# First-layer scores in the spare PSUM bank of the second layer's running state

## The chip, the cores and the metric

The kernel runs on one core of one Trainium2 chip. The metric is the time of one execution on the device in microseconds. Five engines matter. TensorE appears twice in the profile: PE is the streaming of a matmul and PEld the loading of its weights, which may overlap the matmul before it. DVE is VectorE, ACT is ScalarE, POOL is GpSimd, and SP issues the transfers. Products are written to PSUM, and here only ACT and DVE read them from there.

## The reference, cut to what matters

Four layers follow one another on 2048 tokens of width 576: attention A, experts B, A again, B again, with the same weights both times.

```
x = x + A(layernorm(x));  x = x + B(layernorm(x))      # "layer 0" of the kernel
x = x + A(layernorm(x));  x = x + B(layernorm(x))      # "layer 1" of the kernel

A:  q, k, v = x @ wqkv, 32 heads of 18;  pq, pk = phi(q), phi(k)
    kv = sum over tokens of pk (x) v;  z = sum over tokens of pk      # the running state
    o = (pq @ kv) / (pq . z);  return o @ wo
B:  q1, q2 = halves of x @ w_q (32 heads);  s1, s2 = q1 @ k1, q2 @ k2   # 8 scores each
    expert = (argmax s1, argmax s2), one of 64;  act = gelu(x . u[expert])
    return sum over heads of act * v[expert]
```

A is linear attention: its state `kv` needs keys and values of all tokens before the first output. The experts' scores are linear in x, so the kernel folds `w_q` with the keys once and gets the scores of a token by one product with a 576 x 512 matrix.

## The kernel before, in words

The tokens are cut into 16 tiles of 128. Every product of the big matrices is done in three parts, high x high, high x low and low x high, so an input is first transposed on TensorE and then split: ACT copies the high part out of PSUM (`thi`, L110), DVE subtracts it from the original for the low part (`tlo`, L111). The last letter of a name tells whose input it is: `thib`/`tlob` for the experts, `thif`/`tlof` for the next attention, `thio`/`tloo` for the attention's output.

For each token tile the pieces of a layer are small Python generators, and the order in which they run is written out by hand, first as a text that `play` reads, then for tiles 5 to 12 as a loop over `step2`, then as a text again. `in_order` makes this the order of each of PE, ACT, DVE and POOL. In the middle of the program the second half of layer 0 and the first half of layer 1 are interleaved. One `step2(s)` does on PE, in this order:

- `ppk`, `ppv` (L220): keys and values of layer 1, tile s-3
- `ptb` (L205): transposes of the experts' input of tile s and of the chosen experts' weights `cg` of tile s-1
- `ptf` (L205): transposes of layer 1's input of tile s-2
- `kva` (L291): 20 small products that add tile s-3 to layer 1's running state
- `pto` (L205): transposes of the attention's output of tile s+1
- `pps` (L444): the scores of tile s, 14 products of 512 columns, of which 5 have `thib` and `shi`, 4 `thib` and `slo`, and the last 5 `tlob` and `shi`
- `po` (L528): the experts' output of tile s-1
- `ppo` (L414): the attention's output product of tile s+1

`exp_scores` (L437 to L450) holds the scores: it takes a PSUM tile, runs the 14 products into its first 512 columns, and ACT copies these to `s` in SBUF (L449).

All PSUM tiles come from one pool of four slots. A slot is 1024 floats per partition, that is two banks of 512. The tile framework gives a new tile a slot that is free in its own order, and makes the new tile's first product wait until all readers of the slot's last tile have finished. `kva[1]`, the running state of layer 1, is allocated by `front_state(1, 0)` and kept until `state_mask(1)` has read it; its products touch columns 0 to 323, so the second bank of its slot is never written. While it lives three slots rotate among the other tiles. In `step2` eight tiles pass through three slots, so each takes the slot of the tile three before it: `pps` that of `ptb`, `po` that of `ptf`, `ppo` that of `pto`, and the next `ppk` that of `pps`.

Of the kernel before, what the change touches and what calls it, by code (L numbers as in the profile page):

```python
# [39 lines left out]
def blocks(rem):  # L40

    rows, at = [], 0
    for b in range(NB):
        rows.append((at, b - (b > rem)))
        at += 64 if b == rem else P
    return rows


def passes(rem):
    rest = [b for b in range(NB) if b != rem]  # L50
    return ([("hi", b, "hi") for b in range(NB)] + [("hi", b, "lo") for b in rest]
            + [("lo", b, "hi") for b in range(NB)])
# [6 lines left out]
def network(ctx, tc, x_in, wqkv, wo, wq_t, k_t, u_t, v2, c_mask, c_mask4, c_ident, c_code, c_code1, c_scale, c_shift, out):  # L59
# [7 lines left out]
    def psum(name):  # L67
        return ps.tile([P, 1024], F32, tag="ps", name=name)
# [165 lines left out]
    kva = {}  # L234
# [202 lines left out]
    def exp_scores(l, t):  # L437
        n = f"{l}_{t}"

        hl = tt.pop(("b", l, t))  # L440
        p = psum("pps" + n)
        todo = passes(REM)
        for i, (a, b, w) in enumerate(todo):
            nc.tensor.matmul(p[:, :512], hl[a == "lo"][:, b, :], shi[:, b] if w == "hi" else slo[:, blocks(REM)[b][1]],  # L444
                             start=(i == 0), stop=(i == len(todo) - 1))
        s = wk.tile([P, D], F32, tag="s", name="s" + n)
        nc.gpsimd.memset(s[:, :NE], 0.0)
        yield
        nc.scalar.activation(s[:, NE:], p[:, :512], AF.Copy)  # L449
        tt["s", l, t] = s  # L450
# [220 lines left out]
    wl, mk, zs, M = wo_load, state_mask, state_sum, state_fold  # L671
    ld, num, oT, O = back_load, back_scale, back_oT, back_out
    S, sel, gel, po = exp_scores, exp_select, exp_gelu, exp_out
    L = NT - 1

# [187 lines left out]
```

## Time and profile before

| | us |
|---|---|
| median of 3 runs (lowest to highest) | 747.09 (745.76 to 747.62) |
| profiled execution | 748.71 |
| its span, first to last instruction | 746.9 |
| PE busy / PEld busy in the span | 726.5 / 675.2 |
| DVE / ACT / POOL busy | 458.9 / 289.7 / 200.4 |
| granted TensorE clock, mean | 0.995 of full speed |

Layer 1's state is alive from about 298 us (first `kva` product of layer 1) to 533 us. The loop over `step2` takes from 309 to 451 us; one step is 17.7 us. In a row of a view `kva<-ek,v` is the tile written and the tiles read, `x5` the number of instructions put together, and the bracket at the end the time for which the engine stood idle before it and what ended that. Matmul ends are modelled from sizes, so starts are more exact than ends. The profile leaves out layer and tile numbers: `pps` is the scores of any tile.

### The profile page before, as it was taken

How to read it: one execution, taken by the hardware profiler on the slowest of the kernel's cores; microseconds unless marked ns; L12 is line 12 of the kernel's file. 1: busy time of each engine (PE TensorE's matmuls, PEld its weight loads, DVE VectorE, ACT ScalarE, POOL GpSimd, SP SyncE). 2: the span in 40 equal slices, each digit the busy share in tenths (PEclk: the TensorE clock that was granted, in tenths of full speed). 3: DMA queues.
4: the chain of work that ended last, by engine and by line, in shares of the span. 5: the costliest groups of instructions: out<-in, count | busy, mean ns of one | idle time of the engine just before them, and what ended most of it. 6: DMA issues, size and time to landing. Idle time of an engine off the chain costs nothing.

```text
span 746.9 us, 14647 instructions
## 1 busy us (share of the span) xinstructions
PE 726.5 (97%) x5672; PEld 675.2 (90%) x5672; DVE 458.9 (61%) x1006; ACT 289.7 (39%) x588; POOL 200.4 (27%) x541
## 2 busy tenths in 40 slices
PE   7999999999999999999999999999999999999995
PEld 4999999999998889999999999999899999999884
DVE  3732332324236887666666666563366899999986
ACT  4523232332324544444444444452233333444343
POOL 2110001000003543333333333130033334533431
PEclk9999999999999999999999999999999999999998
DMA  9727546641121321222333212222634323121101
GB/s 256 251 81 247 197 159 216 232 130 50 49 64 32 111 99 68 99 86 83 89 104 105 87 68 84 84 72 68 176 87 119 104 83 116 32 88 41 48 33 65
DMA packets 52470, 79.64 MB, mean 107 GB/s; under 512 B 5616, under 2 KB 22512, under 8 KB 52400
## 3 DMA queue, kind: packets, MB, share of 16 engines
q1 hardware_dynamic: 52400, 78.70, 33.1%
q8 instruction: 45, 0.74, 0.4%
q14 instruction: 25, 0.20, 0.1%
HBM read 55.12 MB, written 23.56 MB: 105 GB/s over the span
## 4 chain that ended last, share of the span: by engine, by line
PE 82%; DVE 10%; ACT 3%; issue 2%; POOL 1%; DMA 1%; SPq 0%; DVEq 0%; POOLq 0%; ACTq 0%
PE ppk L220 15%; PE ppv L220 15%; PE ppq L220 13%; PE ppo L414 13%; PE pps L444 12%; PE kva L291 3%; PE fold_ps L560 2%; PE ptb L205 2%; PE ptf L205 2%; PE pto L205 2%; PE po L528 2%; DMA wst<-in_wqkv 1%; PE m L345 1%; DVE o L392 1%; DVE tlob L111 1%
## 5 line engine op out<-in xcount | busy, mean ns | idle before, releaser
L227 DVE TENSOR_SCALAR ek<-ek 128x576 f32<-128x576 f32 x32 | 15.1, 472 | 82.5 <-ACT ek L226 82.5
L220 PE MATMUL ppk<-whi,thif 128*128 128x252 f32 x320 | 50.3, 302 | 2.4 <-ACT thif L110 2.3
L220 PEld LDWEIGHTS ppk<-whi,thif 128*128 128x128 f32 x320 | 44.6, 191 | 6.8 <-ACT thif L110 3.4
L414 PE MATMUL ppo<-ohi,thio 126*128 126x252 f32 (+1 forms) x320 | 50.2, 299 | 0.1
L171 POOL TENSOR_SCALAR rsf<-mvf 128x1 f32<-128x1 f32 x16 | 3.1, 192 | 171.2 <-DVE mvf L169 171.0
L220 PE MATMUL ppk<-whi,tlof 128*128 128x252 f32 x320 | 48.2, 295 | 0.3 <-DVE tlof L111 0.3
L227 DVE TENSOR_SCALAR eq<-eq 128x576 f32<-128x576 f32 x32 | 15.6, 488 | 52.5 <-ACT eq L226 52.5
L220 PE MATMUL ppv<-whi,thif 128*128 128x252 f32 x320 | 47.4, 294 | 0.1
L220 PE MATMUL ppv<-whi,tlof 128*128 128x252 f32 x320 | 46.9, 293 | 0.0
L195 ACT ACTIVATE yb<-x,rsb 128x640 f32<-128x640 f32 x32 | 29.5, 923 | 44.3 <-POOL rsb L188 44.2
L444 PE MATMUL pps<-shi,thib 128*128 128x512 f32 x160 | 43.9, 404 | 2.0 <-ACT thib L110 2.0
L414 PEld LDWEIGHTS ppo<-ohi,thio 126*128 126x128 f32 (+1 forms) x320 | 44.8, 189 | 1.1 <-DVE eq L228 0.3
L220 PEld LDWEIGHTS ppk<-whi,tlof 128*128 128x128 f32 x320 | 44.9, 190 | 0.5 <-DVE tlof L111 0.5
L220 PEld LDWEIGHTS ppv<-whi,thif 128*128 128x128 f32 x320 | 43.9, 188 | 0.4 <-ACT thif L110 0.3
L220 PEld LDWEIGHTS ppv<-whi,tlof 128*128 128x128 f32 x320 | 43.9, 188 | 0.0
L181 ACT ACTIVATE junk<-x,mb 128x576 bf16<-128x576 f32 x32 | 24.7, 771 | 49.5 <-POOL mb L180 46.1
L444 PE MATMUL pps<-shi,tlob 128*128 128x512 f32 x160 | 42.7, 397 | 0.0
L449 ACT ACTIVATE s<-pps 128x512 f32<-128x512 f32 x32 | 19.1, 596 | 54.9 <-PE pps L444 54.9
L251 ACT ACTIVATE v<-ppv 128x252 f32<-128x252 f32 x64 | 20.9, 379 | 50.0 <-PE ppv L220 50.0
L220 PE MATMUL ppq<-whi 128*128 128x252 f32 (+1 forms) x260 | 39.6, 299 | 0.6 <-DVE eq L228 0.6
L404 DVE SCALAR_TENSOR_TENSOR x<-po,x 128x576 f32<-128x576 f32 x29 | 21.9, 753 | 29.3 <-PE po L528 28.3
L414 PE MATMUL ppo<-olo,thio 126*128 126x252 f32 (+1 forms) x256 | 39.5, 293 | 0.0
(155 smaller groups left out, 1788.9 us busy)
## 6 DMA issues: line engine op xcount, KB each, us to landing
fold<-in_wq_t SPq DMA_DIRECT2D x64, 288.0 KB, 4.8
whi<-hl_d SPq DMA_DIRECT2D x26, 320.0 KB, 3.4
pq_d<-eq SPq DMA_DIRECT2D x19, 288.0 KB, 2.2
pq<-pq_d SPq DMA_DIRECT2D x19, 288.0 KB, 3.1
xf<-in_x SPq DMA_DIRECT2D x16, 288.0 KB, 5.4
x<-in_x SPq DMA_DIRECT2D x16, 288.0 KB, 2.7
x_d<-x SPq DMA_DIRECT2D x16, 288.0 KB, 3.3
x<-x_d SPq DMA_DIRECT2D x16, 288.0 KB, 2.7
```

What stands on the lines that cost most here:

```text
L181: nc.scalar.activation(junk, xt, AF.Square, bias=m[:, 0:1], accum_out=m[:, 1:2])
L195: nc.scalar.activation(y, x2, AF.Identity, scale=rs[:, 0:1], bias=rs[:, 1:2])
L205: nc.tensor.transpose(pt[:, b * P:(b + 1) * P], x, ident)
L220: nc.tensor.matmul(o[:, at:at + c1 - c0], tt[a == "lo"][:, b, :], wb[:, cols + c0:cols + c1], start=(i == 0), stop=(i == len(todo) - 1))
L227: nc.vector.tensor_scalar(e, e, 1.0, EPS, op0=ALU.min, op1=ALU.add)
L251: nc.scalar.activation(vt[:, c:c + 4, :63], x.rearrange("p (c e) -> p c e", c=4), AF.Copy)
L291: nc.tensor.matmul(a[64 * h:64 * h + 64, c * 72:c * 72 + n], vt[:, 2 * c + h], fk[:, f0:f0 + n], start=(t == 0 and c == 0), stop=(t == NT ...
L404: nc.vector.scalar_tensor_tensor(y, row(p), 0.0, xt, op0=ALU.add, op1=ALU.add, accum_out=total)
L414: nc.tensor.matmul(p[:, at:at + c1 - c0], hl[a][:r, b], w[:r, c0:c1], start=(i == 0), stop=(i == len(todo) - 1))
L444: nc.tensor.matmul(p[:, :512], hl[a == "lo"][:, b, :], shi[:, b] if w == "hi" else slo[:, blocks(REM)[b][1]], start=(i == 0), stop=(i == l ...
L449: nc.scalar.activation(s[:, NE:], p[:, :512], AF.Copy)
L528: nc.tensor.matmul(p[:, at:at + c1 - c0], c[i], vmix[:, c0:c1], start=(i == 0 and not based), stop=(i == 1))
```

## The change

In `exp_scores` the PSUM tile is no longer always taken from the pool. For layer 0, while the state of layer 1 is alive, the 512 columns are the second half of the state's own tile.

```diff
@@ -438,7 +438,7 @@ def exp_scores(l, t):
         hl = tt.pop(("b", l, t))
-        p = psum("pps" + n)
+        p = kva[1][:, 512:] if l == 0 and 1 in kva else psum("pps" + n)
         todo = passes(REM)
```

This concerns the scores of tiles 4 to 15 of layer 0; those of tiles 0 to 3 and all of layer 1 take a slot as before. In `step2` seven tiles now pass through the three slots. The instructions and their order are the same on all engines. Slots differ between the scores of tile 4 and layer 1's values of tile 14, and agree again from there. What differs are the semaphores for which PE instructions wait.

PE in `step2(6)`, before, from `pto` of tile 7 to the first products of `ppo` of tile 7. The word in brackets names the engine whose semaphore is waited for; a number after a tile's name is its token tile, and the longer one a buffer number.

```order
L205 MATMUL pto_7_4099<-ident,o_7_3760 128x128 [waits PE_49]
L205 MATMUL pto_7_4099<-ident,o_7_3760 128x128 x4
L444 MATMUL pps_6_4110<-shi,thib_6_4072 128x512 [waits DVE_49]
L444 MATMUL pps_6_4110<-shi,thib_6_4072 128x512 x4
L444 MATMUL pps_6_4110<-slo,thib_6_4072 128x512 x4
L444 MATMUL pps_6_4110<-shi,tlob_6_4073 128x512 x5
L528 MATMUL po_5_4132<-vmix,thib_6_4072 128x252 [waits DVE_49]
L528 MATMUL po_5_4132<-vmix,thib_6_4072 128x324
L528 MATMUL po_5_4132<-vmix,tlob_6_4073 128x252
L528 MATMUL po_5_4132<-vmix,tlob_6_4073 128x324
L414 MATMUL ppo_7_4167<-ohi,thio_7_4105 128x252 [waits DVE_49]
L414 MATMUL ppo_7_4167<-ohi,thio_7_4105 128x324
```

The same place in the changed kernel:

```order
L205 MATMUL pto_7_4097<-ident,o_7_3759 128x128 [waits PE_49]
L205 MATMUL pto_7_4097<-ident,o_7_3759 128x128 x4
L444 MATMUL kva_3582<-shi,thib_6_4070 128x512 x5
L444 MATMUL kva_3582<-slo,thib_6_4070 128x512 x4
L444 MATMUL kva_3582<-shi,tlob_6_4071 128x512 [waits DVE_49]
L444 MATMUL kva_3582<-shi,tlob_6_4071 128x512 x4
L528 MATMUL po_5_4129<-vmix,thib_6_4070 128x252 [waits PE_49]
L528 MATMUL po_5_4129<-vmix,thib_6_4070 128x324
L528 MATMUL po_5_4129<-vmix,tlob_6_4071 128x252
L528 MATMUL po_5_4129<-vmix,tlob_6_4071 128x324
L414 MATMUL ppo_7_4164<-ohi,thio_7_4103 128x252 [waits DVE_49,Activation_49]
L414 MATMUL ppo_7_4164<-ohi,thio_7_4103 128x324
```

The wait for DVE has moved from the first score product to the tenth, the first that reads `tlob`. Before, it stood at the first one because the slot was that of `ptb`, which DVE reads last when it makes `tlob`. `po` takes the slot of `ptb` now and `ppo` that of `ptf`, so the first product of `ppo` waits for DVE (the slot) and for ACT (`thio`) in place of DVE alone. (The first product of `ptb` waits for DVE and ACT in both kernels.)

The other place where a wait is new is PE after `ppo` of tile 5, ahead of `step2`: before,

```order
L414 MATMUL ppo_5_3665<-olo,tloo_5_3618 128x252 [waits Pool_49]
L414 MATMUL ppo_5_3665<-olo,tloo_5_3618 128x324
L291 MATMUL kva_3582<-ek_1_3562,v_1_87 64x72 x8
L291 MATMUL kva_3582<-ek_1_3562,v_1_87 64x36 x2
L220 MATMUL ppk_2_3762<-whi,thif_2_3651 128x252 [waits DVE_49,Activation_49]
```

and in the changed kernel:

```order
L414 MATMUL ppo_5_3664<-olo,tloo_5_3618 128x252 [waits Pool_49]
L414 MATMUL ppo_5_3664<-olo,tloo_5_3618 128x324
L291 MATMUL kva_3582<-ek_1_3562,v_1_87 64x72 [waits Activation_49]
L291 MATMUL kva_3582<-ek_1_3562,v_1_87 64x72 x7
L291 MATMUL kva_3582<-ek_1_3562,v_1_87 64x36 x2
L220 MATMUL ppk_2_3761<-whi,thif_2_3650 128x252 [waits DVE_49,Activation_49]
```

The state's products of tile 1 now wait for ACT's copy of the scores of tile 4, since both are in one tile. Over the whole program PE has 589 rows with such a wait in place of 580.

## The prediction

> **What bounds the kernel now.** The first view is the page's busy times, the second the table of stretches, here cut to the length of one step (start:end, length, then busy us and instructions of PE, PEld, DVE, ACT, POOL, the granted clock, and the share and rate of DMA).
>
> ```profile
> PE 726.5 (97%) x5672; PEld 675.2 (90%) x5672; DVE 458.9 (61%) x1006; ACT 289.7 (39%) x588; POOL 200.4 (27%) x541
> ```
>
> ```profile
> 337.70:355.40 17.70, 17.70 (x140) 16.63 (x139) 11.54 (x27) 7.91 (x17) 6.29 (x17) 1.00 0.28 87
> ```
>
> TensorE bounds the place that the change touches: in a step PE is busy 17.70 of 17.70 us at full clock, DVE 11.54, ACT 7.91. By this column nothing can be gained. But a matmul's modelled end hides a short wait behind it, so I read PEld, and there the list of waits (who waited for whom: us in total, times, longest):
>
> ```profile
> PEld kva L291 <- issue: 5.0, 30, 0.2
> ...
> PEld pps L444 <- DVE tlob L111: 1.5, 7, 0.2
> ```
>
> The second row is the one that counts: seven times the weight load of the first score product waited 0.2 us for DVE's `tlob`, which that product does not read. The timeline of one step shows it (start, length, instruction, idle before it). PEld, then PE, then ACT, then DVE:
>
> ```profile
> 336.34 0.53 PEld L205 LDWEIGHTS pto<-ident,o 128*128 128x128 f32 x5
> 337.08 1.00 PEld L444 LDWEIGHTS pps<-shi,thib 128*128 128x128 f32 x5 [0.21 <-DVE tlob L111]
> ```
>
> ```profile
> 330.62 1.46 PE L220 MATMUL ppv<-whi,thif 128*128 128x252 f32 x10
> 331.92 1.20 PE L220 MATMUL ppv<-wlo,thif 128*128 128x252 f32 x8
> 332.96 1.47 PE L220 MATMUL ppv<-whi,tlof 128*128 128x252 f32 x10
> 334.26 0.71 PE L205 MATMUL ptb<-ident,yb 128*128 128x128 f32 x5
> ...
> 336.35 0.77 PE L205 MATMUL pto<-ident,o 128*128 128x128 f32 x5
> 337.09 1.44 PE L444 MATMUL pps<-shi,thib 128*128 128x512 f32 x5
> 338.36 1.10 PE L444 MATMUL pps<-slo,thib 128*128 128x512 f32 x4
> 339.30 1.34 PE L444 MATMUL pps<-shi,tlob 128*128 128x512 f32 x5
> 340.47 0.43 PE L528 MATMUL po<-vmix,thib 128*128 128x252 f32 x2
> ...
> 341.01 1.48 PE L414 MATMUL ppo<-ohi,thio 126*128 126x252 f32 x10
> ...
> 343.37 1.20 PE L414 MATMUL ppo<-ohi,tloo 126*128 126x252 f32 x8
> ...
> 344.67 1.46 PE L220 MATMUL ppk<-whi,thif 128*128 128x252 f32 x10
> ...
> 354.78 1.44 PE L444 MATMUL pps<-shi,thib 128*128 128x512 f32 x5
> ```
>
> ```profile
> 335.12 0.81 ACT L110 ACTIVATE thib<-ptb 128x768 fp32r<-128x768 f32 x1
> ...
> 337.15 0.71 ACT L110 ACTIVATE thio<-pto 128x640 fp32r<-128x640 f32 x1 [0.50 <-PE pto L205]
> 340.67 0.60 ACT L449 ACTIVATE s<-pps 128x512 f32<-128x512 f32 x1 [2.82 <-PE pps L444]
> ```
>
> ```profile
> 335.41 0.76 DVE L392 TENSOR_TENSOR o<-pq,r 128x576 f32<-128x576 f32 x1
> 336.08 0.95 DVE L111 TENSOR_TENSOR tlob<-ptb,thib 128x768 fp32r<-128x768 f32 x1
> 336.95 0.81 DVE L111 TENSOR_TENSOR tlof<-ptf,thif 128x640 fp32r<-128x640 f32 x1
> 337.89 0.82 DVE L111 TENSOR_TENSOR tloo<-pto,thio 128x640 fp32r<-128x640 f32 x1
> ```
>
> `tlob` ends at 336.08 + 0.95 = 337.03, and `pps` starts at 337.09. Its own inputs were there long before: `thib` ended at 335.93.
>
> **The change part by part.** *The wait at the scores.* What it costs is seen against the scores of tile 14, where five transposes also stand between 20 `kva` products and `pps`, and nothing holds the scores up:
>
> ```profile
> 480.38 0.77 PE L205 MATMUL ptf<-ident,yf 128*128 128x128 f32 x5
> 480.90 1.41 PE L444 MATMUL pps<-shi,thib 128*128 128x512 f32 x5
> 482.15 1.10 PE L444 MATMUL pps<-slo,thib 128*128 128x512 f32 x4
> ```
>
> From the transposes' start to the sixth score product it takes 482.15 - 480.38 = 1.77 us there, and 338.36 - 336.35 = 2.01 us in the step above: 0.24 us for the wait and the refilling after it. That stands in seven steps (the count of the waits row, tiles 6 to 12). Tile 5 is the first of the loop:
>
> ```profile
> 318.76 0.76 PE L205 MATMUL pto<-ident,o 128*128 128x128 f32 x5
> 319.39 1.44 PE L444 MATMUL pps<-shi,thib 128*128 128x512 f32 x5
> 320.67 1.10 PE L444 MATMUL pps<-slo,thib 128*128 128x512 f32 x4
> ```
>
> 1.91 us, so 0.14 us too much. Together 7 x 0.24 + 0.14 = 1.8 us on the engine that sets the end. The bounds are the plain idle of the waits row, 1.5 us, and the whole difference of starts: `pto` to `pps` 0.74 us, against 0.47 us from `pto` to `ppv` here, eight times, 2.2 us.
>
> ```profile
> 454.46 0.71 PE L205 MATMUL pto<-ident,o 128*128 128x128 f32 x5
> 454.93 1.57 PE L220 MATMUL ppv<-whi,thif 128*128 128x252 f32 x10
> ```
>
> I take 1.8, since it compares like with like.
>
> *Tile 4* gains nothing: its scores wait for `thib` itself.
>
> ```profile
> 300.32 1.44 PE L444 MATMUL pps<-shi,thib 128*128 128x512 f32 x5 [0.70 <-ACT thib L110]
> ```
>
> Tiles 13 to 15 gain nothing either; the waits row has no more than the seven.
>
> *The waits that take its place.* The tenth score product now waits for `tlob`. Without the stall it starts 0.24 earlier, at 339.06, and `tlob` is done at 337.03: 2.0 us to spare. `po` needs the slot of `ptb`, free at the same 337.03. `ppo` needs `thio` (337.86) and the slot of `ptf` (`tlof`, 337.76) at 340.77: 2.9 us to spare, and `tloo` (338.71) for its products from 343.13. `ppk` needs the slot of `pto`, 338.71, at 344.43. Before, it waited for the copy of the scores, done at 341.27. So each slot is free earlier than before or well before its use.
>
> *More instructions that wait.* Some seven first products of `ppo` wait for two engines in place of one, and a few more for work that PE itself did long before. `ptb` shows what two waits cost: from the last ten `ppv` products to `ptb` it is 334.26 - 332.96 = 1.30 us, the same as between the first ten and the next (331.92 - 330.62). So nothing, as PE's queue has them ready before. If each of the seven cost what the stall did, 1.7 us would be lost again; I take zero, since the row is the same kind of wait.
>
> *The second bank.* The state's products and the scores write different banks of one slot. A `kva` group that comes after scores must wait for ACT's copy, as the order ahead of `step2` shows. There:
>
> ```profile
> 303.91 0.60 ACT L449 ACTIVATE s<-pps 128x512 f32<-128x512 f32 x1 [3.04 <-PE pps L444]
> ```
>
> ```profile
> 308.55 0.81 PE L291 MATMUL kva<-ek,v 128*64 128x72 f32 x20
> ```
>
> The copy ends 4.0 us before. In `step2` the margin is a large part of a step. No cost.
>
> *What the other engines do with it.* Once the stall is gone, `o` from DVE is the next to be late: it ends at 336.17, 0.18 us before `pto`. It does not get later, because what feeds it starts from PE: ACT stood idle 2.82 us before the copy of the scores, until PE had finished them, and all that follows in the step hangs on that copy or on `po`. If PE finishes the scores 0.24 earlier, so does the rest.
>
> *After the loop* the lead has to last for 300 us. PE stays the engine that sets the pace until the tail, so a lead is not lost in a wait for another engine:
>
> ```profile
> 550.00:600.00 50.00, 50.00 (x356) 47.94 (x355) 34.11 (x72) 17.65 (x34) 17.73 (x45) 1.00 0.34 100
> ...
> 650.00:700.00 50.00, 50.00 (x342) 47.07 (x342) 46.88 (x111) 20.01 (x39) 20.27 (x55) 1.00 0.19 60
> ```
>
> DVE's 46.88 of 50 is work that comes with PE's products and moves with them. DMA is at 0.34 or less, so loads are not what would hold it.
>
> **The sum.** The profiled execution took 748.71 us; without 1.8 it is 746.9. It lies 1.6 above the median of the runs, 747.09, and the same term off that gives 745.3 us. That is 0.24% less, a little inside the 0.3% (2.2 us) that a measurement of this kernel can tell from no change.
>
> **Rivals.** *The other bubble goes too.* PEld stands idle 0.17 us before every `kva` group, in each step alike (5.0 us in 30 times). If lack of slots were behind that as well, another 8 x 0.17 = 1.4 us would go: 743.9. Against it: `kva` needs no slot, having its own, and the same gap stands in the first 200 us, where no scores are computed yet:
>
> ```profile
> PEld kva L291 <- issue: 2.2, 13, 0.2
> ```
>
> The Trainium skill, "Perfetto Trace Analysis", section Optimization Strategy, says that a gap repeating through a stretch can mean that PSUM is short for the next tile; the trace agrees for `pps`, by its releaser, and does not show it for `kva`, which has none. 6 in 100.
>
> *The chain through DVE swallows it.* If `o` came at a rate of its own, PE would reach `pto` too early, use up the 0.18 us once, and stand there in each later step: with the 0.14 of tile 5 a gain of 0.3 us, 746.8. It decides if the chain needs more than 17.45 us for a step. For it: only 0.18 us lie between `o` and `pto`. Against it: the 2.82 us of idle ACT above. 12 in 100.
>
> *Slower: one bank for all scores.* The scores no longer rotate. Should a score group have to wait for ACT's copy of the one before, in line, each of tiles 5 to 15 costs a copy, 0.60 us, so 11 x 0.60 = 6.6 less the 1.8 gained: 751.9. It decides where the copy ends later than the next scores start; in the step it ends at 341.27 and they start at 354.78, 13.5 us later. The same page of the Trainium skill, section Matmuls, is for it: independent groups of matmuls should rotate through different banks, so that reading one out overlaps the next group. Here seven other tiles lie between two groups, so the row outweighs the rule. With what new waits on PE could cost beyond my zero, 5 in 100.
>
> **How the numbers follow.** The forecast, the stall gone and nothing in its place, has 77 in 100. With its bounds (1.5 to 2.2 us) and half the spread of the runs before (745.76 to 747.62, so 0.9) its own range is 744.0 to 746.5; a little under half of it, 37 in 100, lies beyond 0.3%. With the first rival that makes faster 0.43. The rest of the forecast and the chain make 0.52 within 0.3%, and slower is 0.05. The range takes in the first two rivals with a little spread: 743.6 to 747.1.
>
> **What would show it.** In the profile after, the waits row of `pps` (by then named `kva`, L444) for `tlob` is gone; from `pto` to the sixth score product it takes 1.77 us; a step takes 17.45 us; ACT's copy reads `kva`; the first product of `ppo` has no idle before it. I am wrong if PE stands before `pto` in the later steps, if the idle appears before `po` or `ppo`, or if the end of the loop is earlier by 1.8 us and the end of the program is not.

## The result, and the profile after

| | before | changed |
|---|---|---|
| median of 22 runs each, us | 746.73 | 744.25 |
| lowest to highest | 745.76 to 749.07 | 743.57 to 746.67 |
| ratio, 95% interval | | 0.9973 (0.9966 to 0.9979) |
| profiled execution, us | 748.71 | 744.04 |
| its span | 746.9 | 742.2 |

The changed kernel is faster by 0.27%, 2.0 us by the ratio, with an interval of 1.6 to 2.5 us that ends clear of zero. The forecast was 745.3 us with a gain of 1.8.

The two profiled executions are 4.7 us apart, more than the runs. The page's busy times of the changed kernel:

```profile
PE 723.5 (97%) x5672; PEld 673.6 (91%) x5672; DVE 458.6 (62%) x1006; ACT 289.7 (39%) x588; POOL 200.3 (27%) x541
```

No engine has another instruction. PE's busy time is 3.0 us less. Of this, 1.8 lie between `pto` of tile 5 and `pto` of tile 14, where PE is busy all the time in both kernels (135.70 and 133.90 us), because its busy time held the stall; 1.1 lie in the first 35 us and are not the change's. The stretch of one step in the changed kernel (columns as in the prediction):

```profile
337.40:354.85 17.45, 17.45 (x140) 16.60 (x139) 11.54 (x26) 7.89 (x17) 6.31 (x17) 1.00 0.28 89
```

A step of 17.70 us has become one of 17.45, again with PE busy all of it. The busy share did not show the stall before and does not show its going. PEld's list of waits in the changed kernel does (us in total, times, longest):

```profile
PEld kva L291 <- issue: 5.0, 30, 0.2
...
PEld pps L444 <- ACT thib L110: 1.8, 2, 1.2
...
PEld kva L444 <- ACT thib L110: 0.9, 1, 0.9
```

There is no row left in which the scores wait for `tlob`, under `pps` or under the new name `kva`. Tile 4's wait for `thib` stands, as does the gap before the state's own products. PE's timeline of the step that the prediction showed, now in the changed kernel:

```profile
333.26 0.77 PE L205 MATMUL pto<-ident,o 128*128 128x128 f32 x5
333.78 1.41 PE L444 MATMUL kva<-shi,thib 128*128 128x512 f32 x5
335.03 1.10 PE L444 MATMUL kva<-slo,thib 128*128 128x512 f32 x4
335.97 1.33 PE L444 MATMUL kva<-shi,tlob 128*128 128x512 f32 x5
337.14 0.43 PE L528 MATMUL po<-vmix,thib 128*128 128x252 f32 x2
...
337.67 1.50 PE L414 MATMUL ppo<-ohi,thio 126*128 126x252 f32 x10
...
350.72 0.76 PE L205 MATMUL pto<-ident,o 128*128 128x128 f32 x5
351.24 1.40 PE L444 MATMUL kva<-shi,thib 128*128 128x512 f32 x5
```

From the transposes to the sixth score product it takes 335.03 - 333.26 = 1.77 us, where it took 2.01. No row carries an idle time in brackets, neither the tenth product, which now has the wait, nor `po` nor `ppo`. The same place in the first step of the loop:

```profile
315.82 0.76 PE L205 MATMUL pto<-ident,o 128*128 128x128 f32 x5
316.34 1.40 PE L444 MATMUL kva<-shi,thib 128*128 128x512 f32 x5
317.58 1.10 PE L444 MATMUL kva<-slo,thib 128*128 128x512 f32 x4
```

It takes 1.76 us against 1.91 before.

What of the 4.7 us is the change's? One place early in the program, which is the same in both kernels, and the last products of each, first before, then changed (PE's timeline):

```profile
34.96 0.81 PE L291 MATMUL kva<-ek,v 128*64 128x72 f32 x20
...
742.69 0.55 PE L528 MATMUL po<-vmix,tlob 128*128 128x252 f32 x2
```

```profile
32.09 0.81 PE L291 MATMUL kva<-ek,v 128*64 128x72 f32 x20
...
738.00 0.49 PE L528 MATMUL po<-vmix,tlob 128*128 128x252 f32 x2
```

At that early place the changed kernel is already 2.87 us ahead, though nothing has changed up to there. Part of this is the granted clock: up to that place it was 0.95 in the trace before and 1.00 in the changed one, and from 10 to 20 us 0.83 against 1.00. From there to the end it takes 707.73 us before and 705.91 after: 1.82 us less. Counted from `pto` of tile 5 (318.76 before, 315.82 after) to the same last products it is 423.93 against 422.18, 1.75 us less. From `pto` of tile 5 to `pto` of tile 14, the first one after the loop (454.46 and 449.72), it is 135.70 against 133.90, 1.80 us less, and from there to the same last products 288.23 and 288.28. So the lead is made in the loop and lasts the 288 us that follow.

### The profile page after: what moved, and what is told of

Read it like the earlier page. It is cut to its first block, busy times and chain, and to the rows that moved or that the text cites. A ratio compares the mean times of both kernels' runs of the same rounds, so it can differ in the third digit from the quotient of the medians.

```text
span 742.2 us, 14654 instructions
## 1 busy us (share of the span) xinstructions
PE 723.5 (97%) x5672; PEld 673.6 (91%) x5672; DVE 458.6 (62%) x1006; ACT 289.7 (39%) x588; POOL 200.3 (27%) x541
## 4 chain that ended last, share of the span: by engine, by line
PE 82%; DVE 10%; ACT 3%; issue 2%; POOL 1%; DMA 1%; SPq 0%; DVEq 0%; POOLq 0%; ACTq 0%
PE ppk L220 15%; PE ppv L220 15%; PE ppq L220 13%; PE ppo L414 13%; PE pps L444 6%; PE kva L444 5%; PE kva L291 3%; PE fold_ps L560 2%; PE ptb L205 2%; PE ptf L205 2%; PE pto L205 2%; PE po L528 2%; PE m L345 1%; DVE o L392 1%; DVE tlob L111 1%
## 5 line engine op out<-in xcount | busy, mean ns | idle before, releaser
L414 PE MATMUL ppo<-ohi,tloo 126*128 126x252 f32 (+1 forms) x256 | 39.4, 293 | 0.0
L220 PE MATMUL ppk<-wlo,thif 128*128 128x252 f32 (+1 forms) x256 | 39.1, 293 | 0.0
L226 ACT ACTIVATE eq<-ppq 128x576 f32<-128x576 f32 x32 | 20.7, 647 | 46.8 <-PE ppq L220 46.8
```

The lines of the kernel that those rows point to most:

```text
L220: nc.tensor.matmul(o[:, at:at + c1 - c0], tt[a == "lo"][:, b, :], wb[:, cols + c0:cols + c1], start=(i == 0), stop=(i == len(todo) - 1))
L226: nc.scalar.activation(e, row(p), AF.Exp)
L414: nc.tensor.matmul(p[:, at:at + c1 - c0], hl[a][:r, b], w[:r, c0:c1], start=(i == 0), stop=(i == len(todo) - 1))
```

## The experiments

The theory: the slot of `ptb` held the first score product until `tlob` was made; that stood in tiles 5 to 12, for 0.14 us of PE's time in tile 5 and about 0.24 in each of the others, and nothing else of the change matters. The rivals: the gain comes from the changed rotation of slots elsewhere; any position of the wait would do, because it is the number of slots that counts; or the moved wait costs something of its own.

**The loop alone.** Only tiles 5 to 12 go to the second bank:

```diff
-        p = kva[1][:, 512:] if l == 0 and 1 in kva else psum("pps" + n)
+        p = kva[1][:, 512:] if l == 0 and 5 <= t <= 12 else psum("pps" + n)
```

> Only the scores of tiles 5 to 12, those of the loop, go into the state's second bank; tiles 4 and 13 to 15 take a slot again. My theory: the whole gain comes from these eight, so as fast as the changed kernel, 2.0 us (0.27%) under the kernel before, and no weight load of the scores waits for tlob. If the gain came from freer slots around the loop (tiles 4, 13 to 15): less than half of it, under 1 us.

Measured: 744.23 us, ratio to the kernel before 0.9966 (0.9951 to 0.9982). PE's timeline of this kernel, first at tile 4, then in a step:

```profile
297.77 1.43 PE L444 MATMUL pps<-shi,thib 128*128 128x512 f32 x5 [0.70 <-ACT thib L110]
...
334.17 1.41 PE L444 MATMUL kva<-shi,thib 128*128 128x512 f32 x5
335.42 1.10 PE L444 MATMUL kva<-slo,thib 128*128 128x512 f32 x4
```

Tile 4 is back in a slot and waits for `thib` exactly as long as in the other kernels; the steps have no stall. The eight tiles of the loop give the whole gain.

**The rest alone.** The other four tiles, 4 and 13 to 15:

```diff
-        p = kva[1][:, 512:] if l == 0 and 1 in kva else psum("pps" + n)
+        p = kva[1][:, 512:] if l == 0 and 1 in kva and not 5 <= t <= 12 else psum("pps" + n)
```

> The reverse: only tiles 4 and 13 to 15 go into the state's bank. My theory: nothing gained, within 0.1% of the kernel before, and the seven waits of 0.2 us for tlob stand as before. If the slots around the loop matter: 1 us or more faster than before.

Measured: 746.64 us, ratio 1.0001 (0.9991 to 1.0011). Its waits of PEld:

```profile
PEld pps L444 <- DVE tlob L111: 1.5, 7, 0.2
...
PEld kva L444 <- ACT thib L110: 0.9, 1, 0.9
```

The seven waits are all there, and so is the time. Four groups of scores in the second bank neither gain nor cost anything that can be measured. With the first run this adds up: all of it is in the loop.

**The wait put back, with the slots as changed.** The scores stay in the second bank, and the five products that read `tlob` come first in the loop:

```diff
         todo = passes(REM)
+        if l == 0 and 5 <= t <= 12:
+            todo = todo[9:] + todo[:9]
```

> As the changed kernel, but for tiles 5 to 12 the five score products that read tlob are done first and not last. The bank and the seven tiles in three slots stay; only the wait for tlob is back at the first product. My theory: the gain is gone, 1.8 us slower than the changed kernel, 0.0% against the kernel before, and a step takes 17.69 us again. If it were the freer rotation of the slots that helps: as fast as the changed kernel, 0.27% under the kernel before.

Measured: 746.41 us, ratio 1.0000 (0.9988 to 1.0012). Waits of PEld, PE's timeline and the stretch of a step:

```profile
PEld kva L446 <- DVE tlob L111: 1.5, 7, 0.2
```

```profile
333.60 0.77 PE L205 MATMUL pto<-ident,o 128*128 128x128 f32 x5
334.34 1.44 PE L446 MATMUL kva<-shi,tlob 128*128 128x512 f32 x5
335.62 1.34 PE L446 MATMUL kva<-shi,thib 128*128 128x512 f32 x5
```

```profile
333.60:351.29 17.69, 17.69 (x142) 16.62 (x138) 11.54 (x27) 7.90 (x17) 6.28 (x18) 1.00 0.27 88
```

The row of the kernel before has come back with the same total, number and longest wait, now as a wait for data and not for a slot. The gain is gone: the times leave room for 0.9 us either way, and in the trace the loop takes 135.69 us against 135.70 before (the table at the end of this section). Freeing a slot gives nothing by itself here: what gave the 2 us is that the wait for `tlob` stands nine products later.

**`tlob` later, with and without the change.** One more DVE instruction on 128 x 576, whose output nothing uses, stands ahead of `tlob` in the eight steps:

```diff
+LATE = [f"b0_{t}" for t in range(5, 13)]
...
+    late = cp.tile([P, D], F32, name="late")
...
+        if n in LATE:
+            nc.vector.scalar_tensor_tensor(late, zb, 0.0, zb, op0=ALU.max, op1=ALU.add)
```

In the kernel before:

> The kernel before with one more DVE instruction (about 0.75 us, its result is not used) ahead of tlob for tiles 5 to 12. My theory: the scores wait for tlob through their slot, so each of the eight steps gets about 0.75 us longer: 6 us (0.8%) slower than before. If the wait for tlob at the slot were not what holds the scores: under 1 us, since DVE has 6 us to spare in a step.

Measured: 752.61 us, ratio 1.0072 (1.0051 to 1.0093), 5.4 us slower. Waits of PEld, then PE and DVE of one step:

```profile
PEld pps L448 <- DVE tlob L113: 6.6, 8, 0.9
```

```profile
333.54 0.76 PE L207 MATMUL pto<-ident,o 128*128 128x128 f32 x5
334.94 1.43 PE L448 MATMUL pps<-shi,thib 128*128 128x512 f32 x5 [0.64 <-DVE tlob L113]
336.21 1.09 PE L448 MATMUL pps<-slo,thib 128*128 128x512 f32 x4
```

```profile
333.27 0.75 DVE L213 SCALAR_TENSOR_TENSOR late<-zb 128x576 f32<-128x576 f32 x1
333.94 0.95 DVE L113 TENSOR_TENSOR tlob<-ptb,thib 128x768 fp32r<-128x768 f32 x1
```

The instruction puts `tlob` off by 0.67 us (333.94 - 333.27). The way to the sixth score product is 336.21 - 333.54 = 2.67 us, 0.66 more than before. Tile 5 loses 0.37, since `tlob` comes only that much later there, so the loop should be 7 x 0.66 + 0.37 = 5.0 us longer, and in the trace it is (140.69 against 135.70). Before the change every bit by which `tlob` was late came out at the end.

In the changed kernel:

> The changed kernel with the same extra DVE instruction. My theory: tlob is needed only at the tenth product, with 2.0 us to spare, so 0.75 us is hidden: as fast as the changed kernel, 0.27% under the kernel before. If the chain through DVE were about to become the bound: 0.75 us a step, about 6 us slower than the changed kernel.

Measured: 744.49 us, ratio to the kernel before 0.9970 (0.9959 to 0.9980). The stretch of a step and its score products:

```profile
333.90:351.35 17.45, 17.45 (x141) 16.60 (x139) 12.09 (x28) 7.89 (x17) 6.68 (x18) 1.00 0.29 89
```

```profile
333.87 0.77 PE L207 MATMUL pto<-ident,o 128*128 128x128 f32 x5
...
335.64 1.10 PE L448 MATMUL kva<-slo,thib 128*128 128x512 f32 x4
```

DVE is busier (12.09 us in place of 11.54), and the step is 17.45 us long all the same, with 335.64 - 333.87 = 1.77 us to the sixth product. Five us of cost in one kernel are nothing in the other. Together with the run before these two, in which the bank and the slots of the change gave nothing, this leaves the place of the wait as what counts.

**How much is hidden.** Four such instructions in place of one, in the changed kernel:

```diff
+            for _ in range(4):
+                nc.vector.scalar_tensor_tensor(late, zb, 0.0, zb, op0=ALU.max, op1=ALU.add)
```

> The changed kernel with four of the extra DVE instructions, about 3.0 us. My theory: 2.0 us are hidden, and the tenth score product waits for the rest, about 1 us in each of eight steps: 8 us slower than the changed kernel, with the idle in the middle of the scores (ahead of the products that read tlob). If the chain through DVE bound already: 3 us a step, 24 us. If the margin were larger than I read: nothing.

Measured: 753.58 us (one run), 9.3 more than the changed kernel's median. Waits of PEld, then PE and DVE of one step:

```profile
PEld kva L449 <- DVE tlob L113: 10.5, 8, 1.4
```

```profile
334.40 0.77 PE L207 MATMUL pto<-ident,o 128*128 128x128 f32 x5
...
338.19 1.43 PE L449 MATMUL kva<-shi,tlob 128*128 128x512 f32 x5 [0.93 <-DVE tlob L113]
339.46 0.43 PE L533 MATMUL po<-vmix,thib 128*128 128x252 f32 x2
```

```profile
334.14 3.13 DVE L214 SCALAR_TENSOR_TENSOR late<-zb 128x576 f32<-128x576 f32 x4
337.19 0.95 DVE L113 TENSOR_TENSOR tlob<-ptb,thib 128x768 fp32r<-128x768 f32 x1
```

`tlob` is put off by 337.19 - 334.14 = 3.05 us. The tenth score product starts 338.19 - 334.40 = 3.79 us after `pto`, against 335.97 - 333.26 = 2.71 in the changed kernel, 1.08 later. So 3.05 - 1.08 = 2.0 us were hidden, which is the slack read from the timeline. The first `po` is 5.06 us behind `pto` in place of 3.88, that is 1.18 later: 0.10 more than the wait itself. In tile 5 the step is 0.78 us longer (18.22 against 17.44), so the loop should be 7 x 1.18 + 0.78 = 9.0 us longer. In the trace it is (142.94 against 133.90); the single run gave 9.3.

**Tile 4's own wait.** Its scores wait for `thib`, which on ACT stands behind the copies of tile 1's values that the state's products read. ACT's timeline there in the changed kernel:

```profile
295.87 0.63 ACT L251 ACTIVATE v<-ppv 128x252 f32<-128x252 f32 x2
296.39 0.23 ACT L253 ACTIVATE v<-ppv 128x72 f32<-128x72 f32 x1
296.51 0.82 ACT L110 ACTIVATE thib<-ptb 128x768 fp32r<-128x768 f32 x1
```

In the experiment, with the rest as in the changed kernel, the piece with these copies (`v1.1x2` in the written order) comes behind `thib`:

```diff
-            bc0.4,3 st1.0 po0.2 v1.1x2 num0.5 num0.6 bc0.4,3 oT0.5 ...
+            bc0.4,3 st1.0 po0.2 num0.5 num0.6 bc0.4,3 v1.1x2 oT0.5 ...
```

> The changed kernel, with the three ACT copies of layer 1's values of tile 1 (v) moved behind the copy that makes thib of tile 4. The one wait that the change left at the scores, 0.70 us for thib at tile 4, should shrink since thib starts about 0.65 us earlier on ACT: 0.6 us (0.08%) faster than the changed kernel, 0.35% under the kernel before. If the next late input takes its place there: no difference from the changed kernel.

Measured: 744.06 us, ratio 0.9966 (0.9954 to 0.9978). PE's timeline at tile 4, in the changed kernel and in this one:

```profile
294.37 0.77 PE L205 MATMUL ptb<-ident,yb 128*128 128x128 f32 x5 [0.35 <-ACT yb L195]
...
297.38 1.44 PE L444 MATMUL kva<-shi,thib 128*128 128x512 f32 x5 [0.70 <-ACT thib L110]
```

```profile
297.26 0.77 PE L205 MATMUL ptb<-ident,yb 128*128 128x128 f32 x5 [0.34 <-ACT yb L195]
...
299.61 1.44 PE L444 MATMUL kva<-shi,thib 128*128 128x512 f32 x5
```

From `ptb` to the scores it is 2.35 us in place of 3.01: 0.66 less, by the same kind of reading as the change itself. The lead reaches the loop: from the early `kva` place of the result section (34.98 us here) to `pto` of tile 5 it takes 283.07 us, against 283.68 to 283.80 in all the other traces, and the loop is as long as in the changed kernel. Whether the time gets shorter by it the runs do not settle: the two medians are 0.2 us apart and the intervals of the two ratios overlap nearly whole.

**The loop in all traces.** One trace of each kernel, from the start of `pto` of tile 5 to that of `pto` of tile 14; the scores of tiles 5 to 12 lie between:

| kernel | `pto` of tile 5 | `pto` of tile 14 | between, us |
|---|---|---|---|
| before | 318.76 | 454.46 | 135.70 |
| changed | 315.82 | 449.72 | 133.90 |
| the loop alone | 316.20 | 450.04 | 133.84 |
| the rest alone | 316.14 | 451.84 | 135.70 |
| the wait put back | 316.02 | 451.71 | 135.69 |
| `tlob` later, kernel before | 315.58 | 456.27 | 140.69 |
| `tlob` later, changed kernel | 316.43 | 450.33 | 133.90 |
| four instructions, changed kernel | 316.18 | 459.12 | 142.94 |
| state's copies later | 318.05 | 451.93 | 133.88 |

The kernels with the stall need 135.7 us and those without it 133.8 to 133.9. This is sharper than the times, in which the runs of one kernel differ by more than the change.

## Why the prediction was right

- **The stall and its releaser.** "The second row is the one that counts" held. The row is gone after the change, stays where the loop's scores keep their slots, and comes back in full when the products that read `tlob` are put first.
- **Its price.** 7 x 0.24 + 0.14 = 1.8 us was read against tile 14, the same products without a stall. Measured: 2.01 to 1.77 in a step, 1.91 to 1.76 in tile 5, 17.70 to 17.45 for the whole step, 1.80 for the loop, 1.75 to 1.82 from trace to trace, and 2.0 (1.6 to 2.5) in the times. The idle alone, 1.5 us, would have been a little low: each of the seven steps loses 0.03 us beside its idle of 0.21, and the 0.14 of tile 5 is not among the seven waits.
- **Tile 4 and tiles 13 to 15 give nothing.** Ratio 1.0001 for these alone.
- **The moved wait has 2.0 us to spare.** In the trace after, `tlob` ends here (DVE's timeline, the step shown above):

```profile
332.31 0.76 DVE L392 TENSOR_TENSOR o<-pq,r 128x576 f32<-128x576 f32 x1
332.99 0.95 DVE L111 TENSOR_TENSOR tlob<-ptb,thib 128x768 fp32r<-128x768 f32 x1
```

  That is 333.94, and its products start at 335.97. A delay of 0.67 us cost nothing, one of 3.05 cost what lay above 2.0.
- **More instructions that wait cost nothing.** `ppo`, which now waits for two engines, follows `po` without idle, and the step got shorter by the full 0.24 us. The bound of 1.7 us is excluded.
- **`o` from DVE does not become the bound, but the prediction misread it.** The rival in which it swallows the gain (746.8) falls: `pto` has no idle before it and the step is 17.45 us long. The `o` that ends 0.18 us before `pto` (0.19 in the changed kernel, 333.07 against 333.26) is, however, not the one that this `pto` reads. `step2(s)` finishes `o` of tile s+2 on DVE and transposes that of tile s+1, so the `o` that `pto` reads at 336.35 in the kernel before was made one step earlier:

```profile
317.43 0.76 DVE L392 TENSOR_TENSOR o<-pq,r 128x576 f32<-128x576 f32 x1
```

  It was done at 318.19, 18.2 us ahead. So `o` was not the next to be late, and the 0.18 us was no margin; the forecast itself does not use it.
- **The other bubble stays.** `kva L291` has the same 5.0 us in 30 times. The forecast of 743.9 falls with it. The Trainium skill, "Perfetto Trace Analysis", section Optimization Strategy, offers a lack of PSUM as one reading of a repeating gap; of two such gaps here it was right for the one that had a releaser.
- **One bank for all scores costs nothing.** ACT's copy of the scores in the changed kernel:

```profile
337.33 0.60 ACT L449 ACTIVATE s<-kva 128x512 f32<-128x512 f32 x1 [2.57 <-PE kva L444]
```

  It ends at 337.93, and the next scores start at 351.24, 13.3 us later; 751.9 falls. The same page of the Trainium skill, section Matmuls, asks for independent groups of matmuls to rotate through banks. The trace shows the limit of that: where the copy has long ended before the next group, a bank that is always the same costs nothing.
- **The absolute time** came out 1.0 us lower than forecast. 0.4 of it is the base: 747.09 was the median of 3 runs, 746.73 is that of 22. The rest is the difference of the medians, 2.5 us, against the 1.8. The ratio says 2.0, and its interval holds 1.8, so whether there is a further gain of some tenths is not settled.

The change lies at the edge of what was called measurable: 0.27%, with an interval of 0.21 to 0.34%. With 22 runs it could be told from nothing; that it is above 0.3% is not shown.

## What to carry to other kernels

When an engine is busy in the whole of a stretch, look at what its weight loads wait for: a short wait repeated in every step hides behind the modelled end of the matmul ahead, and is priced by the distance of starts against a place without the wait. A tile's slot carries a dependence of its own: its first writer waits for the last reader of the tile before, even if it needs nothing that this reader makes, and giving the tile a place of its own moves that wait to the first instruction that really needs the data. What then counts is not the freed slot but how much later the wait stands; a product order that puts the late operand last was worth nothing here as long as the slot waited for the instruction that makes this operand.

## What was not expected of the hardware

- Two executions differ by 2.9 us before 35 us of the program, where the kernels are the same (32.09 against 34.96 in the rows above). The granted clock up to there was 0.95 in the slower one and 1.00 in the other. The difference is more than the change is worth, so two profiled spans alone would have given 4.7 us for a change of 2.
- A DVE instruction of 0.75 us put the next one off by 0.67 us only. Four of them in a row, which write the same tile, put it off by 3.05: if the last one cost 0.67 as well, the other three took 0.79 each (an estimate from these two figures).
- After a wait of 0.93 us on PE, in the run with four instructions, the work behind it came another 0.10 us later.
